# Batch 0's scores from two matmuls a block on keys and maxima in place, a fourth exponentials' buffer, value sums in another bank, and a new written order

## The chip, the cores and the metric

One core of a Trainium2 chip runs the kernel. The time is the device time of one launch in microseconds (us); lower is better. The engines named below are TensorE (PE in the profile, with its weight loads as PEld), VectorE (DVE), ScalarE (ACT), GpSimd (POOL) and SyncE (SP), whose queue starts every DMA here.

## The reference

Two stages follow each other, in float32, on 4 batches, 8 heads, 768 positions, head width 64:

```python
k_sum = k.reshape(B, H, nb, 32, D).max(axis=3)        # maxima of blocks of 32 keys
v_sum = v.reshape(B, H, nb, 32, D).mean(axis=3)       # means of blocks of 32 values
scores_l = scale * q @ k.T, kept where |i - j| < 16   # local window
scores_s = scale * q @ k_sum.T + log(32)              # 24 block scores
a = softmax over [scores_l, scores_s]
x = a @ [v, v_sum]                                    # to 4 x 768 x 512
theta = x @ w_theta
y = w_tok_r @ (x * cos(theta)) + w_tok_i @ (x * sin(theta))
u = x + y
out = u + max(u @ w_ch, 0)
```

Queries, keys, w_theta and w_tok_i are multiplied by 8 first, and the four weight matrices arrive as float64 and are turned into float32 on the core.

## The kernel before, in words

There are 24 attention tiles (4 batches of 6 tiles of 128 positions). A tile is two groups g of 64 positions. A group sees a row of NK = 118 keys: first NB = 24 block maxima, then NL = 94 neighbouring keys.

For a tile the steps are: `scores` (matmuls named s<-k,q, line 522: 16 matmuls of 64x64 weights and 118 columns, 32 instructions in the profile since a float32 matmul is two); the softmax in `att_half` (line 558 on DVE with the mask, line 562 exponentials on ACT); `turn` (line 571, sixteen transposes of the exponentials into banks pa0 and pa1, whose copies of line 577 fill two more buffers of tag "e"); `products` (line 545, exponentials times values v, 32 instructions); `norm_half`; `turn_tile` (line 604, four transposes of the tile into bank t, copied out to x); `theta_tile` (line 635 for batch 0 in whole float32, line 640 later in split halves xh, xl), sine and cosine on ACT, and the multiplication with the tile (line 670, only DVE). `mix_step` (line 698) and `mix_fast` (line 813) multiply by the token weights, and `out_batch` (line 918) by w_ch.

In batch 0 the rows of 118 keys are put together on the core: `copy` (line 499, on ACT or POOL) copies for each tile the 94 keys of each group and the 24 maxima from ks into a buffer k, of which there are two. In the later batches a DMA (k<-kg) brings the keys and only the first two tiles copy maxima. The block means of the values are summed on PE for batch 0 (line 449, x<-vn, into bank pa0), go to a buffer vs on ACT (line 472), and from there by four copies a batch (line 494) into the four v buffers.

Five matmuls on an idle buffer (line 378, t<-zu) stand in the PE queue's first part; nobody reads their result.

The order of all instructions on all engines is written out: `ORDER` is a list of operation numbers, and a letter behind a number chooses the engine (p, a, d, g for PE, ACT, DVE, POOL). Each engine runs its own part of that list in order. `SWITCH` and the other costs in `Program` served to find the order and are not read when the kernel is built.

## Time and profile before

| what | us |
|---|---|
| median of 3 runs | 438.94 (438.0 to 439.17) |
| the profiled execution | 436.4 |
| its span, from the first to the last event | 434.7 |
| TensorE busy in it | 423.7 (97%) |
| DVE, ACT, POOL busy | 357.9, 282.0, 187.8 |

The profiled execution is 1.7 us longer than its span, and 2.5 us below the median of the runs. TensorE is busy nearly all the time, so the profile is read for the few places where it waits and for what its instructions cost next to each other. The granted clock of TensorE is over 90% in each of the profile's 40 slices.

### The profile page before, as it was taken

The page shows a single profiled execution, that of the slowest core. Times are in us where ns is not written, and L with a number is a line of the kernel's source. Part 1 is how long each engine was busy: PE and PEld are TensorE (multiplying, and loading weights), DVE is VectorE, ACT ScalarE, POOL GpSimd, SP SyncE. Part 2 cuts the span into 40 slices and gives each one's busy share as a digit, 9 for nine tenths or more (in the row PEclk, how much of TensorE's full clock was granted, in tenths as well). Part 3 has the DMA queues.
Part 4 walks back from the last instruction along what each step waited for, and adds up shares of the span by engine and source line. Part 5 has one row for each costly group of instructions (what it writes and reads, how often), then busy time and mean ns, then how long its engine had stood idle before and what let it go on. Part 6 is the DMA issues. An engine that isn't in the chain of part 4 may idle for free.

```text
span 434.7 us, 10048 instructions
## 1 busy us (share of the span) xinstructions
PE 423.7 (97%) x3682; PEld 350.2 (81%) x3682; DVE 357.9 (82%) x958; ACT 282.0 (65%) x616; POOL 187.8 (43%) x193
## 2 busy tenths in 40 slices
PE   6999999999999999999999999999999999999996
PEld 1465565566888888888888898999899899999996
DVE  4899999878687597867667987576888999999996
ACT  1899988686685697868396683588944355554330
POOL 2536311678873425257242555451362220253361
PEclk9999999999999999999999999999999999999999
DMA  7999977978975877786779978772368598300357
GB/s 309 385 352 315 340 258 255 255 231 253 301 256 146 247 226 225 225 239 197 205 245 287 285 226 244 246 235 93 112 221 334 166 335 273 99 18 2 109 199 255
DMA packets 76320, 100.06 MB, mean 230 GB/s; under 512 B 23024, under 2 KB 58864, under 8 KB 76272
## 3 DMA queue, kind: packets, MB, share of 16 engines
q1 hardware_dynamic: 76272, 99.43, 71.3%
q8 instruction: 29, 0.48, 0.5%
q14 instruction: 19, 0.16, 0.1%
HBM read 75.82 MB, written 23.59 MB: 229 GB/s over the span
## 4 chain that ended last, share of the span: by engine, by line
PE 80%; DMA 9%; DVE 7%; ACT 2%; issue 1%; SPq 1%; POOL 0%; POOLq 0%; DVEq 0%; ACTq 0%
PE m L813 20%; PE m L698 17%; PE t L640 11%; PE c L918 7%; PE m L918 6%; PE pa L545 5%; PE s L522 4%; DMA v<-vg 2%; PE pa L571 2%; PE t L604 2%; DMA wt<-wtr 2%; DMA q<-qg 1%; PE t L635 1%; DVE f L408 1%; DMA k<-kg 1%; DMA f<-kT 1%
## 5 line engine op out<-in xcount | busy, mean ns | idle before, releaser
L813 PE MATMUL m<-wt,hl 128*128 128x384 f32 x504 | 96.0, 339 | 1.5 <-ACT hl L308 0.8
L813 PEld LDWEIGHTS m<-wt,hl 128*128 128x128 f32 x504 | 88.0, 188 | 5.2 <-ACT hl L308 1.1
L698 PE MATMUL m<-wt,hl 128*128 128x512 f32 (+1 forms) x432 | 84.3, 340 | 0.0
L698 PEld LDWEIGHTS m<-wt,hl 128*128 128x128 f32 x432 | 68.6, 188 | 10.7
L562 ACT ACTIVATE e<-e,st 128x118 f32<-128x118 f32 x192 | 63.5, 388 | 13.6 <-DVE st L558 12.9
L317 POOL TENSOR_TENSOR hl<-zu,hl 128x512 fp32r<-128x512 f32 x24 | 32.5, 1354 | 45.9 <-DVE st L588 15.4
L558 DVE CUSTOM_DVE_ANT_0 e<-s,cs 128x118 f32<-128x118 f32 x192 | 45.6, 272 | 5.1 <-PE s L522 3.2
L640 PE MATMUL t<-wth,xh 128*128 128x512 f32 x144 | 45.8, 399 | 0.0
L670 DVE TENSOR_TENSOR zu<-xn,zu 128x512 f32<-128x512 f32 x48 | 36.9, 780 | 2.4 <-ACT zu L664 2.2
L698 PE MATMUL m<-wt,zu 128*128 128x512 f32 (+1 forms) x96 | 32.8, 488 | 0.0
L726 POOL TENSOR_TENSOR f<-f 128x192 f32<-128x192 f32 x25 | 16.2, 650 | 35.9 <-DMA f<-f_scratch 8.2
L308 ACT CAST hl<-zu 128x512 fp32r<-128x512 f32 x30 | 18.5, 618 | 20.0 <-PE m L813 13.0
L545 PEld LDWEIGHTS pa<-v,e 118*64 118x64 f32 x768 | 24.7, 137 | 6.9 <-issue 2.5
L698 PEld LDWEIGHTS m<-wt,zu 128*128 128x128 f32 x96 | 17.9, 190 | 14.8 <-issue 13.4
L545 PE MATMUL pa<-v,e 118*64 118x65 f32 x768 | 28.1, 224 | 0.9 <-ACT e L577 0.7
L653 DVE SCALAR_TENSOR_TENSOR zu<-zu,t 128x512 f32<-128x512 f32 x24 | 16.4, 682 | 15.3 <-ACT zu L651 15.3
L726 POOL TENSOR_TENSOR zu<-zu 128x512 f32<-128x512 f32 x16 | 21.5, 1348 | 16.5 <-DVE zu L726 9.5
L640 PE MATMUL t<-wth,xl 128*128 128x512 f32 x72 | 28.4, 395 | 0.0
L317 DVE TENSOR_TENSOR hl<-zu,hl 128x512 fp32r<-128x512 f32 x36 | 27.5, 765 | 0.3 <-ACT hl L308 0.2
L651 ACT ACTIVATE zu<-t,bmagic 128x512 f32<-128x512 f32 x24 | 16.5, 687 | 17.3 <-PE t L640 15.5
L522 PE MATMUL s<-k,q 64*64 64x118 f32 x768 | 25.6, 268 | 2.2 <-DMA q<-qg 1.6
L577 ACT COPY e<-pa 118x512 f32<-118x512 f32 x29 | 16.4, 585 | 16.8 <-PE pa L571 16.5
(181 smaller groups left out, 897.2 us busy)
## 6 DMA issues: line engine op xcount, KB each, us to landing
wt<-s_scratch SPq DMA_DIRECT2D x48, 384.0 KB, 4.7
v<-vg SPq DMA_DIRECT2D x48, 195.0 KB, 4.9
s_scratch<-f SPq DMA_DIRECT2D x24, 384.0 KB, 3.5
k<-kg SPq DMA_DIRECT2D x18, 376.0 KB, 5.2
q<-qg SPq DMA_DIRECT2D x24, 256.0 KB, 5.1
wt<-wti SPq DMA_DIRECT2D x6, 768.0 KB, 10.8
wt<-wtr SPq DMA_DIRECT2D x6, 768.0 KB, 10.2
f<-kT SPq DMA_DIRECT2D x12, 384.0 KB, 4.0
```

Of the source, the lines that this page charges most:

```text
L308: nc.scalar.copy(dst(), src())
L317: lambda e: V[e].tensor_tensor(dst(), src(), hi().bitcast(F32), op=ALU.subtract), reads, writes, due, port=BOTH)
L522: mm(0.79 * len(pairs) / NP, [lambda p=p, g=g, h=h: nc.tensor.matmul(sc[h].get()[ROW[g], p], q.get()[ROW[h], p, ROW[g]], k.get()[ROW[h], p ...
L545: mm(2 * 0.433 + scores[0] + (0.2 if scores[0] else 0.0), [lambda n=n, g=g, a=a: nc.tensor.matmul(xa[a].get()[ROW[g], n], turned[g].get()[ ...
L558: op({"DVE": 0.205}, lambda eng, n=n: nc.vector.tensor_tensor_reduce(e()[:, n], sc[n % 2].get()[:, 2 * a + n // 2], mask(m), -SCALE, 3.0e3 ...
L562: op({"ACT": 0.288}, lambda eng, n=n: nc.scalar.activation(e()[:, n], e()[:, n], AF.Exp, bias=st.get()[:, n:n + 1], scale=-1.0), [(st, n)] ...
L640: calls = [lambda t=t, xx=xx, k=k, c=c: nc.tensor.matmul(th.get(), xx.get()[:, c], w_th[c].get()[:, k], start=(c == 0 and t == 0), stop=(c ...
L670: op({"DVE": c_dve(DM, "two")}, lambda e, z=z, hc=hc: nc.vector.tensor_tensor(z(), xn[b, i].get().rearrange("p h d -> p (h d)")[:, None, h ...
L698: nc.tensor.matmul(acc[th](), zz, w[:, TT[th]], start=(s == 0 and r == 0 and t == 0 and (th == 0 or c == 0)), stop=(s == NT - 1 and r == 1 ...
L726: lambda e: V[e].tensor_tensor(dst(), x(), y(), op=ALU.add if sign > 0 else ALU.subtract), reads, writes, due, port=BOTH)
L813: calls = [lambda ref=ref, tt=tt, z=z, s=s, j=j, t=t, x=x, k=k, bank=bank, first=first: nc.tensor.matmul(bank[j].get()[:, :HT], z.get()[:, ...
L918: calls = [lambda k=k, t=t, x=x, y=y: nc.tensor.matmul(to.get(), weights[n][x][0]()[:, k, j * P:(j + 1) * P], operands[n].get()[:, y, k], ...
```

## The change

In batch 0 no buffer k is filled. A block of scores (one pair of heads, one group) comes from two matmuls: one reads the 94 keys where the DMA put them, and one reads the 24 maxima in ks; they write the two column ranges of the same row in the score bank. There are 32 matmuls a tile instead of 16, in batch 0's six tiles alone.

The buffer vs is gone: the means go straight into the first v buffer, and three copies a batch fill the others. Its place goes to a fourth buffer of tag "e". Batch 0's value sums are accumulated in the mixing bank m0 instead of pa0. From the seventh tile on `turn_tile` reads the bank t once (to x), and xh and xl are made from x in SBUF. Two steps may now run on a second engine: rounding theta on DVE, and the multiplication with the tile on POOL. `ORDER` is a new list; in it half of the 48 multiplications of line 670 have gone to POOL.

```diff
 ORDER = """
-8 31 23 0g 17 18 25 27 29 1 24 2 9 39 86 10 26 3 44 28 30 4 32 33 46 45g 47g 50 5 19 35 49 6 48g 7g 87d 51 79 11g 60 12 185 61
...
+0g 15 1g 79 8g 23 2 17g 3 9 80 39 25 31 27 29 81g 33 18 19 82 83 11g 20 24 4 35 26 10 12 5 28 30 21 6g 7 43 32 22 72 44 45 53
...
-            A1=13, T1=10, PREP=5, QB=2, VSPE=1, VB=4, KB=2, STR=2, WARM=5, SP0=1, FUSE=99, RELOAD=2, RT=6, RM=6, XA=6, XB=2, ZU=5, HL=4, EB=3, TAU_A=8.2, TAU_M=4,
+            A1=13, T1=10, PREP=5, QB=2, VSPE=1, VB=4, KB=2, STR=2, WARM=5, SP0=1, FUSE=99, RELOAD=2, RT=6, RM=6, XA=6, XB=2, ZU=5, HL=4, EB=4, TAU_A=8.2, TAU_M=4,
...
-            pv = Ref(ps, [P, NP, P], tag="pa0")
+            pv = Ref(*((pm, [P, DM], F32, "m0") if b == 0 else (ps, [P, DM], F32, "pa0")))
...
-        vs = Ref(apool, [NB, H, DV], tag="vs")
+        vbuf[b] = [Ref(apool, [NB + VL, H, DV], tag="v", bufs=K["VB"]) for _ in range(K["VB"])]
+        first = vbuf[b][0]
...
-            if 2 * i + g < K["VB"]:
+            if 0 < 2 * i + g < K["VB"]:
...
-            if i < K["KB"]:
+            if b > 0 and i < K["KB"]:
                 copy(lambda pp=pp: k.get()[:, pp, :, :NB], lambda pp=pp, n=len(r): ks.get()[:, pp, None].broadcast_to((P, n, 2, NB)), 2 * len(r) * NB,
-            if b == 0:
-                for h in range(r.start // 2, (r.stop + 1) // 2):
-                    for g in range(2):
-                        w = slice((2 * i + g) * QT, (2 * i + g) * QT + NL)
-                        copy(lambda g=g, h=h: k.get()[:, 2 * h:2 * h + 2, g, NB:], lambda h=h, w=w: keys[0][h].get()[:, :, w],
...
         def scores(pairs):
-            mm(0.79 * len(pairs) / NP, [lambda p=p, g=g, h=h: nc.tensor.matmul(
-                sc[h].get()[ROW[g], p], q.get()[ROW[h], p, ROW[g]], k.get()[ROW[h], p, g], start=True, stop=True)
...
+            def block(p, g, h, cols, keys_of):
+                return lambda: nc.tensor.matmul(sc[h].get()[ROW[g], p, cols], q.get()[ROW[h], p, ROW[g]], keys_of(), start=True, stop=True)
...
+                near = [slice((2 * i + g) * QT, (2 * i + g) * QT + NL) for g in range(2)]
+                calls += [block(p, g, h, slice(NB, NK), lambda p=p, g=g, h=h: keys[0][p // 2].get()[ROW[h], p % 2, near[g]]) for g in range(2) for h in range(2)]
+                calls += [block(p, g, h, slice(0, NB), lambda p=p, h=h: ks.get()[ROW[h], p]) for g in range(2) for h in range(2)]
...
-            hi_op(x_h.get, tx.get, DM, [tx], [x_h], due, psum=True)
-            op({"DVE": c_dve(DM)}, lambda e: nc.vector.tensor_tensor(x_l.get(), tx.get(), x_h.get().bitcast(F32), op=ALU.subtract), [tx, x_h], [x_l], due)
+            hi_op(whole, tx.get, DM, [tx], [(x, i)], due, psum=True)
+            hi_op(x_h.get, whole, DM, [(x, i)], [x_h], due, engines=("ACT", "DVE", "POOL"))
+            lo_op(x_l.get, whole, x_h.get, DM, [(x, i), x_h], [x_l], due)
...
-            op({"DVE": c_dve(DM, "two")}, lambda e, z=z, hc=hc: nc.vector.tensor_tensor(
+            op({"DVE": c_dve(DM, "two"), "POOL": c_pool(DM)}, lambda e, z=z, hc=hc: V[e].tensor_tensor(
```

The DMAs that SP starts first, before the change (zu<-kT are batch 0's keys, x<-vn its values for the sums, wth<-wth the theta weights, wt the token weights):

```order
L302 DMA x<-vn 128x2x512
L302 DMA zu<-kT 128x798 x4
L302 DMA q<-qg 128x512
L302 DMA wth_100<-wth 128x1024
L302 DMA x<-vn 128x2x512 x2
L302 DMA wth_150<-wth 128x1024
L302 DMA q<-qg 128x512
L302 DMA v<-vg 96x520 x2
L302 DMA wth_234<-wth 128x1024
L302 DMA wth_238<-wth 128x1024
L302 DMA q<-qg 128x512
```

And the same place in the changed kernel:

```order
L301 DMA wth_80<-wth 128x1024
L301 DMA zu<-kT 128x798
L301 DMA q<-qg 128x512
L301 DMA zu<-kT 128x798
L301 DMA x<-vn 128x2x512
L301 DMA zu<-kT 128x798 x2
L301 DMA x<-vn 128x2x512 x2
L301 DMA wth_155<-wth 128x1024
L301 DMA q<-qg 128x512
L301 DMA wth_197<-wth 128x1024
L301 DMA v<-vg 96x520 x2
L301 DMA q<-qg 128x512 x2
```

A first part of the theta weights now stands ahead of everything; the first values stand behind the second keys; the queries of tile 3 stand right behind those of tile 2, and the last theta weights behind both.

The start of the PE queue before (s<-k,q scores, t<-zu the idle matmuls, pa<-x,vt the value sums):

```order
L378 MATMUL t<-zu 128x512
L449 MATMUL pa_114<-x,vt 24x512 x2
L522 MATMUL s_121<-k,q 64x118
L522 MATMUL s_123<-k,q 64x118
...
L378 MATMUL t<-zu 128x512
L449 MATMUL pa_114<-x,vt 24x512 x4
```

And in the changed kernel:

```order
L377 MATMUL t<-zu 128x512 x4
L521 MATMUL s_133<-zu,q 64x94
L521 MATMUL s_135<-zu,q 64x94
...
L521 MATMUL s_133<-ks,q 64x24
L521 MATMUL s_135<-ks,q 64x24
...
L449 MATMUL m_151<-x,vt 24x512 x2
L377 MATMUL t<-zu 128x512
```

Four of the five idle matmuls now stand ahead of the first scores (one before) and one behind them (four before, all among the first three tiles), and the first two value sums have moved behind the first half of tile 0's scores.

A round of the PE queue in the middle, before, in batch 1 (pa<-cs,e transposes, pa<-v,e products, t<-cs,xn the tile's transposes, m<-wt,hl mixing):

```order
L698 MATMUL m_1474<-wt,hl 128x256
L571 MATMUL pa_1803<-cs,e 118x64
...
L522 MATMUL s_1828<-k,q 64x118
...
L545 MATMUL pa_1850<-v,e 64x65 x8
L545 MATMUL pa_1859<-v,e 64x65 x8
L604 MATMUL t<-cs,xn 128x128 x4
L698 MATMUL m_1491<-wt,hl 128x512
```

And a round of the changed kernel, in batch 2:

```order
L709 MATMUL m_2195<-wt,hl 128x256
L579 MATMUL pa_2650<-cs,e 118x64
...
L709 MATMUL m_2193<-wt,hl 128x512
...
L612 MATMUL t<-cs,xn 128x128 x4
L553 MATMUL pa_2704<-v,e 64x65 x8
L553 MATMUL pa_2713<-v,e 64x65 x8
L521 MATMUL s_2728<-k,q 64x118
...
L709 MATMUL m_2229<-wt,hl 128x512
```

The scores have gone from between transposes and products to behind the products, and six mixing matmuls stand between the transposes of the exponentials and the tile's transposes. Over the whole queue, transposes of exponentials are followed directly by split mixing or theta matmuls at 2 places before and at 13 now.

## Rows read from the trace of the kernel before

**Rows 1.** The page: each engine's busy time, share of the span, instructions.

```profile
PE 423.7 (97%) x3682; PEld 350.2 (81%) x3682; DVE 357.9 (82%) x958; ACT 282.0 (65%) x616; POOL 187.8 (43%) x193
```

**Rows 2.** What TensorE waited for: us in total, times, longest.

```profile
PE s L522 <- DMA q<-qg: 1.6, 1, 1.6
...
PE m L813 <- ACT hl L308: 0.8, 1, 0.8
PE pa L545 <- ACT e L577: 0.7, 3, 0.4
PE s L522 <- POOL k L499: 0.6, 1, 0.6
PE m L813 <- DVE x L822: 0.6, 1, 0.6
PE pa L545 <- DVE e L577: 0.2, 1, 0.2
```

**Rows 3.** Timeline of TensorE's opening: start, length, what, count, wait before.

```profile
9.73 0.64 PE L522 MATMUL s<-k,q 64*64 64x118 f32 x16 [1.58 <-DMA q<-qg]
10.30 1.12 PE L378 MATMUL t<-zu 128*128 128x512 f32 x2
...
12.97 3.62 PE L449 MATMUL pa<-x,vt 128*24 128x512 f32 x8
16.52 1.04 PE L522 MATMUL s<-k,q 64*64 64x118 f32 x32
...
44.14 1.02 PE L698 MATMUL m<-wt,zu 128*128 128x512 f32 x2
```

**Rows 4.** Timeline of TensorE, one round in batch 1.

```profile
118.75 0.68 PE L571 MATMUL pa<-cs,e 64*118 64x64 f32 x16
119.36 1.04 PE L522 MATMUL s<-k,q 64*64 64x118 f32 x32
120.33 1.15 PE L545 MATMUL pa<-v,e 118*64 118x65 f32 x32
...
121.82 3.42 PE L698 MATMUL m<-wt,hl 128*128 128x512 f32 x18
125.08 0.62 PE L640 MATMUL t<-wth,xh 128*128 128x512 f32 x2
...
125.78 1.20 PE L698 MATMUL m<-wt,hl 128*128 128x512 f32 x6
126.81 0.62 PE L640 MATMUL t<-wth,xh 128*128 128x512 f32 x2
```

**Rows 5.** Timeline of TensorE, the two rounds with mixing behind the transposes.

```profile
226.62 0.68 PE L571 MATMUL pa<-cs,e 64*118 64x64 f32 x16
...
231.46 0.62 PE L640 MATMUL t<-wth,xh 128*128 128x512 f32 x2
...
308.87 0.68 PE L813 MATMUL m<-wt,hl 128*128 128x384 f32 x3
309.48 0.68 PE L571 MATMUL pa<-cs,e 64*118 64x64 f32 x16
...
313.49 0.63 PE L640 MATMUL t<-wth,xh 128*128 128x512 f32 x2
```

**Rows 6.** Timeline of ACT: tile 0's first exponential, tile 2's copy to x.

```profile
12.46 0.39 ACT L562 ACTIVATE e<-e,st 128x118 f32<-128x118 f32 x1 [3.10 <-DVE st L558]
...
39.36 0.60 ACT L308 COPY x<-t 128x512 f32<-128x512 f32 x1
```

**Rows 7.** Groups of ACT: shape, count, busy us, mean ns, idle before.

```profile
L499 ACT COPY k<-zu 128x188 f32<-128x188 f32 x7 | 2.2, 341 | 0.6 <-DMA zu<-kT 0.6
```

**Rows 8.** Timeline of DVE: first maxima, first softmax step.

```profile
5.47 0.95 DVE L445 TENSOR_REDUCE ks<-zu 128x24 f32<-128x768 f32 x1 [3.65 <-DMA zu<-kT]
...
12.14 0.28 DVE L558 CUSTOM_DVE_ANT_0 e<-s,cs 128x118 f32<-128x118 f32 x1 [0.71 <-PE s L522]
```

**Rows 9.** The chain that ended last, in its opening: start, length, what.

```profile
3.23 6.37 DMA q<-qg
```

More of the change, by code (lines that the diff above doesn't have):

```diff
@@ L484, in att_tile @@
             kbuf[b] = []
[L485 removed]
         pr.late, pr.key = K["R_KV"], ("KV", b * NT + i)
[L487 removed]
+        x, ks = xt[b], ksum[b]
         q = Ref(apool, [P, NP, P], tag="q", bufs=K["QB"])
@@ L521, in scores @@
         def scores(pairs):
-            mm(0.79 * len(pairs) / NP, [lambda p=p, g=g, h=h: nc.tensor.matmul(
-                sc[h].get()[ROW[g], p], q.get()[ROW[h], p, ROW[g]], k.get()[ROW[h], p, g], start=True, stop=True)
-                for p in pairs for g in range(2) for h in range(2)], [q] + [(k, (x, y)) for x in pairs for y in ("sum", 0, 1)], [(x, y) for x in sc for y in pairs], due, mode="score")
+            def block(p, g, h, cols, keys_of):
+                return lambda: nc.tensor.matmul(sc[h].get()[ROW[g], p, cols], q.get()[ROW[h], p, ROW[g]], keys_of(), start=True, stop=True)
+            calls, rd = [], [q]
+            for p in pairs:
+                if b > 0:
+                    calls += [block(p, g, h, slice(0, NK), lambda p=p, g=g, h=h: k.get()[ROW[h], p, g]) for g in range(2) for h in range(2)]
+                    rd += [(k, (p, y)) for y in ("sum", 0, 1)]
+                    continue
+                near = [slice((2 * i + g) * QT, (2 * i + g) * QT + NL) for g in range(2)]
+                calls += [block(p, g, h, slice(NB, NK), lambda p=p, g=g, h=h: keys[0][p // 2].get()[ROW[h], p % 2, near[g]]) for g in range(2) for h in range(2)]
+                calls += [block(p, g, h, slice(0, NB), lambda p=p, h=h: ks.get()[ROW[h], p]) for g in range(2) for h in range(2)]
+                rd += [(keys[0][p // 2], p), (ks, p)]
+            mm((0.79 if b > 0 else 1.0) * len(pairs) / NP, calls, rd, [(x, y) for x in sc for y in pairs], due, mode="score")
         products()
```

207 lines of the change are left out of this document (105 added, 102 removed).

## The prediction

> **What bounds the kernel now.** The page comes first: TensorE is busy for 423.7 of 434.7 us [rows 1], so at most 11 us of the span are not its work, and some of those are the launch and the last output. The list of its waits comes second [rows 2]: it names one wait for the first queries (1.6), 0.9 in four short waits for the copied transposes, 0.6 for copied maxima before batch 1's first scores, and 0.8 and 0.6 late in the mixing. Nothing else of weight stands there. The third view is the timeline of the opening [rows 3]: first scores at 9.73, tile 1's scores at 16.52, the raw mixing at 44.14. Between 9.73 and 44.14 TensorE also runs four idle matmuls, 1.05 each: 1.12 in the record, less the 0.07 by which a record reaches into the next (9.73 + 0.64 against 10.30). The reader is to see that there is little waiting to remove, that every added microsecond of matmul counts after 44.14, and that before 44.14 TensorE follows ScalarE: tile 0's first exponential is at 12.46 and tile 2's copy to x ends at 39.96 [rows 6], 27.5 us with hardly a gap.
>
> The sum is made against the profiled execution's span of 434.7; its time is 436.4, and the median of the runs shown is 438.94. I add the difference of spans to the median. What a measurement can tell from no change is 0.3%, here 1.3 us.
>
> **The score matmuls.** A tile's 32 score instructions take 0.97 from start to the products' start, eight on each of four quarters of the array, so 0.121 for 118 columns; the transposes take 0.61 for eight on each half, 0.076 for 64 columns [rows 4]. A line through both gives 0.023 plus 0.00083 a column: 0.101 for 94 columns and 0.043 for 24, together 0.023 more than one of 118, and 0.18 more a tile. From below, the columns are as many as before: 0. From above, a 24-column matmul costs no more than the 64-column row, 0.076: 0.45 a tile. I take 0.2, as the line has it. That is 1.0 us in the five tiles before 44.14 and 0.2 in the sixth.
>
> The Trainium skill, page "TensorEngine Tiling (Array Packing)", section "Instruction Overhead", speaks against the split: a matmul has about 60 cycles of overhead and one column takes as long as 60. By that rule the 24 columns would be priced as 60, 0.073 on the same line, and a tile would cost an estimated 0.42 more, 2.5 us in all six instead of 1.2. No row here has a matmul that small, so it is the upper end that the rule leans to.
>
> **The opening.** Batch 0's DMAs arrive one behind the other. Sizes follow from the shapes (399 KB for a 128x798 tensor, 512, 256). The first keys are there at 5.47 [rows 8], with 911 KB; the queries at 3.23 + 6.37 = 9.60 [rows 9], with 2364 KB: 352 KB/us. In the new order the last keys have 2876 KB, so they land at 11.0 instead of about 9, and their maxima (0.95 on DVE, rows 8) are ready at 12.0. The first half of tile 0's scores can start sooner, at about 9.2 (before 9.73), but the softmax takes both halves: it starts at about 13.0 instead of 12.14 [rows 8]. Tile 1's queries are the same number of bytes down the line in both orders (4668 KB, 16.1), so its scores stay near 16.5.
>
> TensorE's own work from the first scores to the mixing was 34.4 minus 0.7 of waits. Three idle matmuls leave it (3.15), two of six value sums come in (half of the four that took 3.55 from 12.97 to 16.52, rows 3: 1.8), the scores add 1.0: 33.3. From 9.2 that would reach 42.5 with no wait at all. ScalarE decides: it loses six copies in this stretch (2.2 for seven [rows 7], so 1.9) and about 0.3 net of small steps, 25.3 instead of 27.5. It begins at 13.2, and then has nothing ready until the value sums end and tile 0's transposes are through; I charge 1.2 for that. Tile 2's copy then ends at 39.7, and with the same 4.2 as before the mixing starts at 43.9. **Term: -0.25**, between -1.6 (no wait) and +0.7 (ScalarE 1 us later). So the copies, which VectorE and GpSimd no longer serve, and the idle matmuls give back little here: what is late next is ScalarE. The fourth buffer costs nothing and lets exponentials start before a product has read the old ones; its cover is that nothing else used that space. The other cost at nothing is the queries of tile 3, now issued right behind tile 2's: they wait for tile 1's scores, and the last theta weights and two v loads stand behind them on SP. Those weights are needed some 8 us later; were that cover gone, theta of tile 0 would start late by the excess.
>
> **The order in the middle.** In a round before the change, transposes, scores, products and the tile's transposes lie in a row between mixing: 118.75 to 125.08 is 6.33, less 18 mixing matmuls at 0.172 (1.03 for six, 125.78 to 126.81) and less the scores' 0.97 leaves 2.26 [rows 4]. Where mixing stood behind the transposes, 309.48 to 313.49 with nine mixing matmuls leaves 2.46, and 226.62 to 231.46 with twelve leaves 2.78 [rows 5]. The new form thus costs 0.20 to 0.52 more a round, and the scores, now behind the products, I add at their plain 0.97. The changed order has 13 such places instead of 2. **Term: 11 x 0.20 = +2.2**; the lower row of the two, since the other one holds a short wait. The new places before 44.14 are none.
>
> The same page of the Trainium skill, section "Key Properties", says that a change of the tiling mode drains TensorE. The rows agree that a change costs: three mixing matmuls before transposes take 0.61 (308.87 to 309.48, rows 5) instead of 0.52. Counted by that rule alone, 112 changes of tile shape become 121, and the term would be an estimated 9 x 0.09 = 0.8 instead of 2.2; I keep whole rounds, since they hold what a drain is not.
>
> **The waits after 44.14.** They sum to 2.2: 0.6 and 0.2 for maxima and transposes, 0.8 and 0.6 late [rows 2]. The first should go: half of the multiplications of line 670 leave DVE, which is the engine that makes the maxima, and batch 1's k buffers no longer wait for batch 0's scores to read them. The 0.2 goes too, since mixing now covers the copies between transposes and products. Of the late 1.4 I leave 0.8: the ring of four hl buffers is as it was, but w_ch matmuls are now mixed in earlier. **Term: -1.4**, between -2.2 and 0.
>
> **The sum.** -0.25 + 0.2 + 2.2 - 1.4 = +0.75: a span of 435.4, and 439.7 for the median of runs. That is within 0.3%.
>
> **Rivals.** *Faster.* The fourth buffer and the lighter ScalarE let TensorE run the opening without a wait: the mixing starts at 42.5 (1.4 sooner than forecast), and the late waits go altogether (0.8 more). That gives -1.45 from before, 437.5. For it speaks that three of the waits in [rows 2] are ScalarE's copies and that it loses 1.8 us of copies; against it, that the softmax starts later and the bytes are the same. Chance 0.27.
>
> *Slower by the order.* Each of the 11 rounds costs 0.52, as the row at 226.62: 3.5 more than forecast, 443.2. From 0.25 a round on, the change is over 1.3 us slower. For it, that it is one of only two rows of this form; against it, that the other reads 0.20. Chance 0.19.
>
> *Slower by the small matmuls.* At 0.45 a tile the sixth tile adds 0.25 and the five others 1.25, of which the waits for ScalarE hide a part, most likely half: +0.9 on the forecast, 440.6; it takes the 0.45 and a wait of ScalarE's that is no longer there to be slower by 0.3%. Chance 0.12.
>
> *No change that a measurement shows,* as summed: 0.42, with its own range of 437.8 to 440.2.
>
> **The numbers.** The cases give faster 0.27, within 0.3% 0.42, slower 0.31. The bounds added up go from -3.9 (mixing at 42.5, 0.8 for the order, no late wait, scores at 0) to +6.6 (mixing at 44.8, 0.52 a round, all late waits, scores at 0.45). I cut both ends, which need every bound at once: 436.2 to 442.8.
>
> **What would show it.** The first scores near 9.2 but the softmax near 13; the raw mixing between 43 and 45. Score groups of batch 0 about 1.15 from start to start instead of 0.97. Rounds with mixing behind the transposes 0.2 longer. No wait for k before batch 1's scores; one late wait for hl. The prediction is wrong if the mixing starts before 42.5 or after 45, if a round of the new form costs under 0.1 or over 0.3 more, if batch 0's scores take over 1.4, or if TensorE waits anew in batches 1 to 3, where it hardly waited.

## The result: 443.75 us, slower by 1.3%

The changed kernel takes 443.75 us (median of 6 runs, 442.13 to 445.15), the kernel before 437.96 on the same chip (6 runs, 436.6 to 439.17): a ratio of 1.0132, interval 1.0104 to 1.016. The forecast of 439.7 with "no change that a measurement shows" was wrong, and its range ended at 442.8. The time is that of the rival "slower by the order" (443.2), but not for its reason, as the runs show.

The first two profiles differ by more than the medians (spans 443.1 and 434.7, 8.4 us), because the one of before fell on one of its fastest executions and that of the changed kernel on the slowest of its six (445.15). Both kernels were therefore profiled again (`b_again`, `a_again`: spans 437.3 and 440.9, 3.6 us). What is said of sizes below goes by this second pair, with the first beside it; the medians differ by 5.8. The page of the changed kernel, first engines, then the queue that brings instructions (packets, MB, share), against [rows 1]:

```profile
span 443.1 us, 10396 instructions
PE 427.8 (97%) x3874; PEld 353.9 (80%) x3874; DVE 362.4 (82%) x961; ACT 279.4 (63%) x579; POOL 191.6 (43%) x195
q8 instruction: 30, 0.49, 0.5%
```

TensorE has 192 matmuls more (6 tiles x 32, a float32 matmul being two) and is busy 4.1 us longer. Its list of waits, which answers to [rows 2]:

```profile
PE pa L553 <- ACT e L585: 2.7, 2, 1.9
...
PE t L612 <- DVE zu L664: 1.6, 2, 0.9
PE m L824 <- issue: 1.0, 1, 1.0
PE s L521 <- DMA k<-kg: 0.7, 1, 0.7
PE m L824 <- ACT hl L307: 0.7, 1, 0.7
PE pa L579 <- ACT xn L601: 0.5, 2, 0.3
PE m L709 <- POOL zu L681: 0.4, 1, 0.4
```

The wait for copied maxima is gone, as forecast. In its place stand waits that the list before does not have: for bank t, which must be read before the next transposes of the tile (zu L664), for normed tiles (xn), for the DMA of keys (0.5 in `b_again` too), and an "issue" of 1.0 in the last mixing, where the engine waits for nothing that the profile names. The opening, to be held against [rows 3]:

```profile
8.12 0.39 PE L521 MATMUL s<-zu,q 64*64 64x94 f32 x8
...
9.47 1.88 PE L449 MATMUL m<-x,vt 128*24 128x512 f32 x4
...
16.56 0.39 PE L521 MATMUL s<-zu,q 64*64 64x94 f32 x8
...
17.80 0.68 PE L579 MATMUL pa<-cs,e 64*118 64x64 f32 x16
...
25.55 0.30 PE L553 MATMUL pa<-v,e 118*64 118x65 f32 x2 [1.93 <-ACT e L585]
...
27.22 2.08 PE L646 MATMUL t<-xh,x 128*128 128x512 f32 x2
29.23 0.59 PE L521 MATMUL s<-zu,q 64*64 64x94 f32 x8
...
31.10 1.12 PE L646 MATMUL t<-xl,x 128*128 128x512 f32 x2
...
35.45 0.66 PE L612 MATMUL t<-cs,xn 128*128 128x128 f32 x4 [0.89 <-DVE zu L664]
...
47.80 7.90 PE L709 MATMUL m<-wt,zu 128*128 128x512 f32 x24
```

First scores stand at 8.12 (forecast 9.2), a tile's scores take 16.56 to 17.80 = 1.24, the mixing starts at 47.80 (forecast 43 to 45). Tile 1's products wait 1.93 for exponentials, and then two theta matmuls take 2.0 instead of about 0.95, and the scores at 29.23 take 1.87. The windows there (length, then PE, weight loads, DVE, ACT, POOL, granted clock, DMA share, GB/s) tell why:

```profile
24.00:26.00 2.00, 0.30 (x2) 0.19 (x2) 1.28 (x7) 1.69 (x4) 0.62 (x1) 1.00 1.10 323
26.00:28.00 2.00, 1.83 (x31) 1.51 (x32) 1.61 (x8) 1.43 (x5) 0.00 (x0) 0.80 0.96 322
28.00:30.00 2.00, 2.00 (x26) 0.78 (x28) 1.17 (x5) 1.58 (x4) 0.60 (x1) 0.50 0.99 391
```

After a stretch in which TensorE worked 0.30 of 2 us its granted clock falls to half, 1.2 instead of 2.4 GHz.

The forecast let ScalarE set the pace of the opening. From its first exponential to the end of its copy of tile 2 to x, ScalarE (ACT, the fourth of the busy times) worked for 26.70 of 27.50 us before and works for 25.21 of 30.10 now:

```profile
12.46:39.96 27.50, 26.70 (x344) 14.92 (x344) 26.38 (x115) 26.70 (x68) 13.82 (x26) 1.00 1.02 342
```

```profile
13.78:43.88 30.10, 25.98 (x474) 16.69 (x474) 25.92 (x105) 25.21 (x61) 6.85 (x10) 0.94 1.00 331
```

So it has less work, and it waits 4.9 us instead of 0.8. Its longest waits here are for loads of weights, 1.73 for theta's (xl) and 1.00 for a token weight (f), and 1.13 are for VectorE. The copies that tile 1's products wait for stand right behind the first of these (24.88):

```profile
24.31 0.67 ACT L399 ACTIVATE xl<-wth 128x512 f32<-128x512 f32 x1 [1.73 <-DMA wth<-wth]
...
43.29 0.59 ACT L307 COPY x<-t 128x512 f32<-128x512 f32 x1
```

The mixing follows the end of that copy by 3.9 us (4.2 before). A round in the middle, which answers to [rows 4]:

```profile
206.40 0.68 PE L579 MATMUL pa<-cs,e 64*118 64x64 f32 x16
207.02 1.31 PE L709 MATMUL m<-wt,hl 128*128 128x512 f32 x6
208.17 0.60 PE L612 MATMUL t<-cs,xn 128*128 128x128 f32 x4
208.70 1.15 PE L553 MATMUL pa<-v,e 118*64 118x65 f32 x32
209.78 1.04 PE L521 MATMUL s<-k,q 64*64 64x118 f32 x32
210.75 1.31 PE L709 MATMUL m<-wt,hl 128*128 128x512 f32 x6
211.90 0.39 PE L651 MATMUL t<-wth,xh 128*128 128x512 f32 x1
```

206.40 to 211.90 is 5.50; less twelve mixing matmuls at 0.172 and 0.97 for the scores it is 2.47, 0.21 more than the 2.26 of the form before.

The second pair, `b_again` and then `a_again`: the first raw mixing; then `a_again`'s longest waits from the mixing to 390 us.

```profile
45.91 4.46 PE L698 MATMUL m<-wt,zu 128*128 128x512 f32 x13
```

```profile
46.82 3.60 PE L709 MATMUL m<-wt,zu 128*128 128x512 f32 x10
```

```profile
PE m L824 <- issue: 1.0, 1, 1.0
PE s L521 <- DMA q<-qg: 0.7, 1, 0.7
PE t L612 <- DVE zu L664: 0.7, 1, 0.7
PE pa L553 <- DMA v<-vg: 0.5, 1, 0.5
```

In `b_again` the waits there are 0.9 for hl, 0.6 each for copied maxima and xl, and 0.5 each for keys and x. In `a_again` ScalarE works for 24.85 of 28.92 us from its first exponential to its copy of tile 2 (13.97 to 42.89), with 2.6 of waits for weights and 1.1 for VectorE.

Of the 3.6 us between the two spans, 0.9 lie before the mixing, 3.4 between it and the last 288 matmuls for w_ch (382.75 before, 387.03 after), and the tail gives 0.7 back. TensorE's waits in the middle sum to 3.16 in `b_again` and 4.10 in `a_again`, so 0.9 of the 3.4 is waiting and 2.4 is longer work. In the first pair it is 3.7, 5.3 (2.3 of it waits, 3.1 work) and -0.6. The work in the middle differs least between the pairs; the opening and the waits vary more from execution to execution.

### The profile page after: what moved, and what is told of

Read it like the earlier page. It is cut to its first block, busy times and chain, and to the rows that moved or that the text cites. A ratio compares the mean times of both kernels' runs of the same rounds, so it can differ in the third digit from the quotient of the medians.

```text
span 443.1 us, 10396 instructions
## 1 busy us (share of the span) xinstructions
PE 427.8 (97%) x3874; PEld 353.9 (80%) x3874; DVE 362.4 (82%) x961; ACT 279.4 (63%) x579; POOL 191.6 (43%) x195
## 4 chain that ended last, share of the span: by engine, by line
PE 73%; DVE 14%; DMA 8%; issue 2%; ACT 1%; SPq 1%; POOL 0%; DVEq 0%; ACTq 0%
PE m L709 17%; PE m L824 17%; PE t L651 10%; PE c L929 7%; PE m L929 5%; PE s L521 5%; PE pa L553 4%; DMA f<-vT 2%; PE pa L579 2%; PE t L612 2%; DVE f L407 2%; DVE wt L410 2%; DMA v<-vg 2%; DMA zu<-kT 1%; DMA f<-kT 1%
## 5 line engine op out<-in xcount | busy, mean ns | idle before, releaser
L709 PE MATMUL m<-wt,hl 128*128 128x512 f32 (+1 forms) x432 | 87.0, 342 | 0.1
L570 ACT ACTIVATE e<-e,st 128x118 f32<-128x118 f32 x192 | 64.5, 388 | 18.2 <-DVE st L566 17.9
L316 POOL TENSOR_TENSOR hl<-zu,hl 128x512 fp32r<-128x512 f32 x25 | 33.8, 1355 | 38.7 <-DVE hl L316 12.5
L681 POOL TENSOR_TENSOR zu<-xn,zu 128x512 f32<-128x512 f32 x24 | 32.2, 1345 | 37.8 <-ACT zu L675 15.6
L709 PE MATMUL m<-wt,zu 128*128 128x512 f32 (+1 forms) x96 | 33.7, 492 | 0.4 <-POOL zu L681 0.4
L553 PEld LDWEIGHTS pa<-v,e 118*64 118x64 f32 x768 | 24.9, 137 | 9.7 <-issue 5.9
L709 PEld LDWEIGHTS m<-wt,zu 128*128 128x128 f32 x96 | 17.5, 190 | 14.5 <-issue 12.2
L737 POOL TENSOR_TENSOR f<-f 128x192 f32<-128x192 f32 x26 | 17.3, 665 | 26.8 <-DVE hl L316 7.9
L307 ACT CAST hl<-zu 128x512 fp32r<-128x512 f32 x28 | 17.0, 617 | 18.9 <-PE m L824 10.4
L651 PEld LDWEIGHTS t<-wth,xh 128*128 128x128 f32 x144 | 24.2, 188 | 2.7 <-issue 0.2
L585 ACT COPY e<-pa 118x512 f32<-118x512 f32 x34 | 19.1, 586 | 8.9 <-PE pa L579 8.9
L664 DVE SCALAR_TENSOR_TENSOR zu<-zu,t 128x512 f32<-128x512 f32 x24 | 16.4, 684 | 7.4 <-ACT zu L662 7.0
```

The lines of the kernel that those rows point to most:

```text
L316: lambda e: V[e].tensor_tensor(dst(), src(), hi().bitcast(F32), op=ALU.subtract), reads, writes, due, port=BOTH)
L553: mm(2 * 0.433 + scores[0] + (0.2 if scores[0] else 0.0), [lambda n=n, g=g, a=a: nc.tensor.matmul(xa[a].get()[ROW[g], n], turned[g].get()[ ...
L570: op({"ACT": 0.288}, lambda eng, n=n: nc.scalar.activation(e()[:, n], e()[:, n], AF.Exp, bias=st.get()[:, n:n + 1], scale=-1.0), [(st, n)] ...
L585: lambda e, t=t, g=g: (nc.scalar.copy if e == "ACT" else nc.vector.tensor_copy)(t.get()[:NK], tp[g].get()[:NK].rearrange("k n q -> k (n q) ...
L651: calls = [lambda t=t, xx=xx, k=k, c=c: nc.tensor.matmul(th.get(), xx.get()[:, c], w_th[c].get()[:, k], start=(c == 0 and t == 0), stop=(c ...
L681: op({"DVE": c_dve(DM, "two"), "POOL": c_pool(DM)}, lambda e, z=z, hc=hc: V[e].tensor_tensor(z(), xn[b, i].get().rearrange("p h d -> p (h ...
```

## The experiments

Three questions: what makes the opening late, what the order costs, and what each edit costs by itself. Each ratio is to the kernel before on the same chip. "The mixing" is the start of the first raw mixing; "later waits" are TensorE's waits from there on, summed.

**The opening.** The theories: a *queue* theory (tile 3's early query load delays the weights and values behind it on SP), a *work* theory (the matmuls there simply take longer, and ScalarE is late), and a *clock* theory (fewer idle matmuls among the first tiles let the granted clock fall). Four kernels ran together; `a_again` is the changed kernel without an edit.

> The changed kernel once more, nothing edited, as the measure for the three runs beside it and for how much of its profile comes back. If the opening's loss belongs to the kernel, the trace again has the wait of about 1.9 us before tile 1's products, the stretch at half clock after it (26.7 to 30.3) and the raw mixing near 47.8. If it was an accident of one execution, the mixing starts near 44 to 45 and the time is still about 443.7, and the loss has to be sought after it.

443.18, ratio 1.010 (1.0072 to 1.0128). The mixing starts at 46.82, and the clock does not fall at all in this execution. So the half clock is not needed for being slower; it comes on top.

`a_q3_later` moves tile 3's query load (274) behind theta weights (93) and values (179, 181) on SP:

```diff
-223 274 93 179 181 100 224
+223 93 179 181 100 274 224
```

> The changed kernel with the load of tile 3's queries moved back behind the last theta weights, two v loads and a token weight on SP's queue; nothing else. Queue theory: this load held SP from 13.6 to 17.9 us, the theta weights behind it landed at 24.3, ScalarE waited for them with tile 1's copies behind, TensorE stood 1.9 + 0.3 us and its clock then halved for 3.7 us (1.85 lost). Without it: no wait over 0.8 before tile 1's products, no half clock, mixing at 44 to 44.7 instead of 47.8, a time 3 to 4 us under the changed kernel's (about 440.3). Rival, clock theory: the missing idle matmuls leave gaps of 0.8 to 0.9 that halve the clock anyway: the wait goes but the half-clock stretch stays, mixing near 46. Rival, ScalarE's pace: mixing not before 47.

445.17, 1.0136 (1.0104 to 1.0167), mixing at 49.92: no gain. The theta weights are issued 4.4 us earlier (13.91 instead of 18.35) but reach ScalarE at 23.63, where the two profiles of the changed kernel have 24.31 and 23.44, so the queue theory fell: their place on SP is not what makes them late. The time alone would not show it, since this profile has other losses: the clock is at half from 26.3 to 29.7, and TensorE stands still inside tile 2's scores, where nothing is missing that another engine makes. Timeline, and the window up to the stall:

```profile
22.08 0.36 PE L521 MATMUL s<-zu,q 64*64 64x94 f32 x5
...
24.66 0.30 PE L521 MATMUL s<-zu,q 64*64 64x94 f32 x2 [2.22 <-issue]
```

```profile
0.00:24.65 24.65, 17.50 (x219) 8.32 (x220) 13.58 (x54) 10.74 (x26) 6.62 (x23) 1.00 0.95 311
```

`a_idle_back` puts the idle matmuls (18 to 22) back among the first three tiles (43, 44 the halves of tile 0's scores, 183 tile 1's, 32 to 36 value sums):

```diff
-18 19 20 21 43 32 22 44 34 36 183 61 62 65 226
+18 43 32 19 44 20 34 36 183 61 62 21 65 22 226
```

> The changed kernel with the five idle matmuls at the places of the kernel before (one in front, one behind each half of tile 0's scores, one behind tile 0's transposes, one behind its products); loads as in the changed kernel. Queue theory alone: the products of tile 1 still wait for ScalarE's copies near 25.5, now with 0.9 less idle time ahead; what is gained is at most the clock. Clock theory: with the gap from 23.6 to 25.5 shortened and the gap before tile 0's products filled, the half-clock stretch goes, mixing near 46.0, the time 1.5 to 2 us lower (about 442). If neither: the idle matmuls only add work, mixing at 48 or later and the time up to 1 us higher.

444.22, 1.0131 (1.0101 to 1.016). From 9.35, its first value sums, TensorE is busy for 18.32 of 18.65 us:

```profile
9.35:28.00 18.65, 18.32 (x274) 9.08 (x276) 12.95 (x64) 10.61 (x29) 2.55 (x5) 1.00 0.90 312
```

Yet the mixing starts at 47.87. The clock column (1.00) counts the time ahead of the trace's first clock record as full, and here that record begins at 12.08. Up to there TensorE ran at the lower level: the four value sums take 3.22, against 1.88 in the changed kernel (9.47 above).

```profile
9.35 3.22 PE L449 MATMUL m<-x,vt 128*24 128x512 f32 x4
```

With three idle matmuls more between the first scores and the mixing (1.05 each), TensorE's gaps are filled, and now ScalarE waits for TensorE: 3.3 of the 28.95 us from its first exponential to its copy of tile 2. So the run trades one wait for another and gains nothing; it does not tell what holds the opening of the changed kernel. Ahead of the window the queries and maxima kept TensorE waiting for 2.0 and 0.9, as the queries did in [rows 3].

`b_idle_front` gives the kernel before the new places of the idle matmuls:

```diff
-18 32 50 19 51 20 34 36 195 68 69 21 72 22 242
+18 19 20 21 32 50 22 51 34 36 195 68 69 72 242
```

> The kernel before with its idle matmuls at the places of the changed kernel (four in front, one between the halves of tile 0's scores). If ScalarE alone sets the opening (my prediction's step), the mixing starts at 44.1 as before, with waits where the idle matmuls stood: time within 0.3% of before. If TensorE's work sets it, the mixing starts up to 3 us sooner. Clock theory: with the idle matmuls gone from between the tiles, the waits lower the granted clock somewhere between 18 and 35 us, and the mixing starts 0.5 to 2 us later.

438.91, 1.001 (0.9992 to 1.0028), mixing at 46.12 (45.91 in `b_again`). TensorE has three idle matmuls less from the first scores to the mixing, and waits 4.9 us there instead of 2.2: its own work does not set that opening. Idle matmuls alone are worth nothing in it.

`a_idle_two`, run later, moves one of them ahead of tile 0's products (65) and one ahead of its transposes (211), behind which TensorE had waited:

```diff
-18 19 20 21 43 32 22 44 34 36 183 61 62 65 226 200 201 211 204
+18 19 43 32 20 44 34 36 183 61 62 21 65 226 200 201 22 211 204
```

> The changed kernel with two of its four front idle matmuls moved: one ahead of tile 0's products, one ahead of tile 0's turned tile, so into the stretch where TensorE waits for ScalarE's copies before tile 1's products (0.5 to 2.2 us in five traces) and the granted clock was at half for 3.4 us or more behind it in four of the five. Clock theory: no stretch at half clock behind it, mixing at 46 to 46.8, time 0.5 to 1.5 lower (442). Rival, work theory: each idle matmul is 1.05 of TensorE's own, and the time is 0.5 to 2 higher (444 to 445) with mixing at 48; so it was with five at the old places, where the clock stayed up and the mixing came at 47.9 all the same.

444.56, 1.0128 (1.0097 to 1.0159). The clock was at half from 9.8 to 13.2 and from 37.1 to 40.5, elsewhere than in the changed kernel, and the mixing started at 50.45. The clock theory's remedy fails.

**The order.** Operations are numbered alike in these kernels, so that the first 263 (about the opening) can be taken from one list and the rest from the other. `a_old_order` has all edits in the order of before, without the removed operations; `a_open_old` takes only the opening from it, `a_rest_old` only the rest.

```diff
 ORDER = """
-0g 15 1g 79 8g 23 2 17g 3 9 80 39 25 31 27 29 81g 33 18 19 82 83 11g 20 24 4 35 26 10 12 5 28 30 21 6g 7 43 32 22 72 44 45 53
+8 31 23 0g 17 18 25 27 29 1 24 2 9 39 79 10 26 3 28 30 4 32 33 43 5 19 35 6 7g 80d 44 72 11g 53 12 178 54 20 57 45 56 46 81g 47
...
```

> All edits of the code (scores from two matmuls in place, no copies of keys, no buffer vs, four exponentials' buffers, value sums in the mixing bank, the bank t read once), but every operation in the place and on the engine that it had in the kernel before; the operations that are gone are left out of the list. Order theory: the new list is the loss, and the edits cost at most the 0.27 us a tile that the trace shows for the scores, of which the five tiles of the opening hide some: 437.5 to 439.5, ratio 0.998 to 1.003. Rival, edits theory: twice as many matmuls, and twice as many instructions to fetch while the DMA queues are full, cost the opening 3 us: 441 or more, with waits named issue before batch 0's scores or products. A third way: six copies less on ScalarE and sixteen less on GpSimd gain what the matmuls cost and more: 436 or less.

> The changed kernel, with its first 263 operations (all that its list has ahead of the mixing) in the order and on the engines of the kernel before; the rest in the new order. If the loss lies in the opening alone (3.7 us by the first two traces), the time is 440 or less, ratio to before 1.000 to 1.004. If it lies in the order behind 44 us (2.7 for rounds, 2.3 for waits by those traces), the time stays at 442.5 to 443.5. If both, near 441.

> The other half: the changed kernel's opening in its new order, and all that follows in the order of the kernel before. If the loss lies in the opening alone: 442 to 443. If it lies in the middle's rounds and waits: 439 or less, and the rounds behind 100 us have the old form at 0.2 us less each. If both halves cost, this run and the one with the old opening share the 5 us between them, and their sum over before comes to the changed kernel's.

> The kernel before once more, nothing edited, for a second profile of it: the first one was of an execution of 436.4, below the median of its runs. If the first trace is typical, the raw mixing again starts near 44.1 and TensorE's waits after it sum to about 2.2. If the opening varies from one execution to the next, the mixing starts between 44.5 and 46.5, and part of the 3.7 us by which the changed kernel's opening seemed later is not the change's.

| kernel | us | ratio (interval) | mixing | later waits |
|---|---|---|---|---|
| b_again | 438.55 | 1.0001 (0.9972 to 1.003) | 45.91 | 3.2 |
| a_old_order | 448.49 | 1.0212 (1.0177 to 1.0248) | 46.15 | 7.4 |
| a_open_old | 443.01 | 1.009 (1.0055 to 1.0125) | 48.14 | 2.9 |
| a_rest_old | 452.62 | 1.0334 (1.0284 to 1.0385) | 46.80 | 11.1 |

This turned the question round. The edits in the order of before cost 2.1%, and the new list takes 0.8 to 1.1 of that back. Nor is the opening the main part: with either opening the new rest gives 0.9 to 1.3%, with the old rest 2.1 to 3.3%. (In the profile of `a_open_old` the clock record begins at 16.38, so its mixing is late by up to 3.1 us for that alone.) So it was to be asked what the edits cost.

**One part each.** `b_rounds` is the kernel before, with one group of six mixing matmuls in 14 rounds moved up behind the transposes of the exponentials, the new form of round. The PE queue at the first of them:

```diff
 L571 MATMUL pa_1393<-cs,e 118x64
-L522 MATMUL s_1421<-k,q 64x118
...
+L698 MATMUL m_1421<-wt,hl 128x512
+L698 MATMUL m_1423<-wt,hl 128x256
...
+L522 MATMUL s_1430<-k,q 64x118
```

> The kernel before, where in 14 rounds (tiles 8 to 16 and 18 to 22) six mixing matmuls are taken from behind the tile's transposes and put between the transposes of the exponentials and the scores; nothing else moves. My prediction's price of this form is 0.20 a round, the upper one 0.52. With 0.20: 14 x 0.20 = 2.8 us slower, 441, ratio 1.005 to 1.008, and each such round reads 0.2 longer in the timeline. With 0.52: 7 us slower. If the tile mode costs nothing by itself and the loss in rounds came from waits: 438 to 439.

466.12, 1.0596 (1.0553 to 1.064). Such a round without waits:

```profile
124.48 0.68 PE L571 MATMUL pa<-cs,e 64*118 64x64 f32 x16
125.08 1.32 PE L698 MATMUL m<-wt,hl 128*128 128x512 f32 x6
126.34 1.04 PE L522 MATMUL s<-k,q 64*64 64x118 f32 x32
...
128.80 1.53 PE L698 MATMUL m<-wt,hl 128*128 128x512 f32 x7
```

```profile
PE t L640 <- DVE xl L610: 7.9, 10, 1.4
PE m L698 <- DVE x L717: 5.4, 3, 2.0
```

124.48 to 128.80 is 4.32, less 1.03 to 1.045 for the six 3.28, where [rows 4] leave 118.75 to 121.82 = 3.07: +0.21, as in the changed kernel. Fourteen such rounds are 2.9 of the 27.9 us between this span and that of `b_again` (465.2 and 437.3). The waits in the middle sum to 20.7, 17.5 more: scores that come 1.25 later make VectorE's queue, which works in its written order, late for what stands behind them. The other 7.5 are longer work, about 3.3 of it the lower clock (0.98 from 45 to 120, 0.97 from 280 to 340); the rest I have not placed. The form of the round costs 0.2, and it can't be had alone: the other engines' lists must be written for it.

`c_old_x` is `a_old_order` with bank t read twice, as before the change; the other edits remain.

```diff
-            whole = lambda: x.get()[:, :, i * P:(i + 1) * P]
-            hi_op(whole, tx.get, DM, [tx], [(x, i)], due, psum=True)
-            hi_op(x_h.get, whole, DM, [(x, i)], [x_h], due, engines=("ACT", "DVE", "POOL"))
-            lo_op(x_l.get, whole, x_h.get, DM, [(x, i), x_h], [x_l], due)
+            hi_op(x_h.get, tx.get, DM, [tx], [x_h], due, psum=True)
+            op({"DVE": c_dve(DM)}, lambda e: nc.vector.tensor_tensor(x_l.get(), tx.get(), x_h.get().bitcast(F32), op=ALU.subtract), [tx, x_h], [x_l], due)
```

> As the run in the old order, but the bank t is read as in the kernel before (xh from the bank, xl as bank minus xh on DVE, x from the bank); the other edits stay. The old order with all edits lost 10 us, nearly all behind 46 us, where DVE's xl and xn end waits that were not there. Theory: the longer chain bank, x, xh, xl (one more step of 0.6 us ahead of theta) is what the old order has no room for: without it 437.5 to 440. Rival: the means written straight into the first v buffer hold that buffer early, so that v loads and the queue behind them come late: the time stays at 444 or more. Where the time falls between, both count.

442.07, 1.0064 (1.0037 to 1.0091), later waits 3.7 instead of 7.4. The single read, which the forecast had not priced, is over half of what the edits cost in this order.

`b_x_once` is that edit the other way, the removed lines above alone put into the kernel before. `b_x_noport`, run later, makes xh and xl without the kernel's rule by which an operation of GpSimd waits for such a step of VectorE ahead of it in the list.

> The kernel before with the third edit alone: the bank t read once into x, xh made from x and xl from x and xh (the two copies take the places of the two that read the bank, in that order; xl follows). The difference of the two runs in the old order says 6.4 us for this edit there. If the longer chain ahead of theta is that cost: 442 to 445, with waits for xl of 0.5 to 1.5 before theta. If the cost came from where that run had put the copies: 438 to 439.5.

> The kernel before with the bank t read once, as in the run with that edit alone (0.95% slower), except that the two operations that now read SBUF no longer count for the kernel's rule by which an operation of GpSimd waits for the DVE operation on SBUF ahead of it in the list. If GpSimd's added wait is what that edit cost (3.2 us for xl ahead of a hl at 282, and TensorE's 1.3 for that hl), the time comes back to within 0.3% of before, 438 to 440. If the longer chain, or the slower operations themselves when GpSimd works beside them (the mean of xl rose from 0.69 to 0.84), are the cost, it stays at 442 to 444.

```diff
-            hi_op(x_h.get, whole, DM, [(x, i)], [x_h], due, engines=("ACT", "DVE", "POOL"))
-            lo_op(x_l.get, whole, x_h.get, DM, [(x, i), x_h], [x_l], due)
+            hi_op(x_h.get, whole, DM, [(x, i)], [x_h], due, psum=True)
+            op({"DVE": c_dve(DM)}, lambda e: nc.vector.tensor_tensor(x_l.get(), whole(), x_h.get().bitcast(F32), op=ALU.subtract), [(x, i), x_h], [x_l], due)
```

443.28, 1.0095 (1.0061 to 1.0129), and 442.02, 1.01 (1.007 to 1.013). The groups of xl in `b_again`, `b_x_once` and `b_x_noport` (count, busy, mean ns, idle before):

```profile
L610 DVE TENSOR_TENSOR xl<-t,xh 128x512 fp32r<-128x512 f32 x18 | 12.3, 686 | 6.7 <-ACT x L308 3.6 <-ACT xh L308 3.1
```

```profile
L317 DVE TENSOR_TENSOR xl<-x,xh 128x512 fp32r<-128x512 f32 x18 | 15.2, 844 | 8.0 <-ACT xh L308 7.5
```

```profile
L612 DVE TENSOR_TENSOR xl<-x,xh 128x512 fp32r<-128x512 f32 x18 | 18.5, 1029 | 7.8 <-ACT xh L308 7.5
```

The subtraction takes 686 ns on the mean with one operand in the bank, 844 with both in SBUF, and 1029 with both in SBUF and without the rule. One by one, the 18 of `b_again` take 659 to 692, with an operation of GpSimd beside them or not. With both operands in SBUF those that no operation of GpSimd overlaps take 677 to 694, no longer than before; among the overlapped ones the longest takes 1825 in `b_x_once` and 2217 in `b_x_noport`. With the rule GpSimd stands instead, and TensorE behind it, in `b_x_once`:

```profile
282.11 1.31 POOL L317 TENSOR_TENSOR hl<-zu,hl 128x512 fp32r<-128x512 f32 x1 [3.23 <-DVE xl L317]
```

```profile
283.47 0.45 PE L816 MATMUL m<-wt,hl 128*128 128x384 f32 x1 [1.33 <-POOL hl L317]
```

Either way 1.0%: without that wait the 18 subtractions take 18.5 us instead of 15.2, and the time stays.

`a_x_twice` puts the two reads into the changed kernel with its own order (the diff of `c_old_x`).

> The changed kernel with the bank t read as in the kernel before (xh from the bank, xl on DVE as bank minus xh, x from the bank), each operation in the place that its successor has in the new list. If the edit costs in the new order what it costs in the old (0.95%, 4 us), the time falls to 439 to 440.5, the best version with the other edits. If the new order was made for it and hides it, the time stays at 443. If the bank, held longer, makes theta late, it rises to 445 and TensorE waits for xl or for the bank before theta and before the turned tiles.

444.21, 1.0118 (1.0077 to 1.0159), mixing 48.01, later waits 2.8. In the new order taking the single read back gains nothing that can be measured: that list hides what it costs.

`b_scores_only` gives the kernel before batch 0's new scores alone, with the 27 copies gone; `b_vs_only` gives it the means in the first v buffer, the fourth "e" buffer and bank m0.

```diff
+                near = [slice((2 * i + g) * QT, (2 * i + g) * QT + NL) for g in range(2)]
+                calls += [block(p, g, h, slice(NB, NK), lambda p=p, g=g, h=h: keys[0][p // 2].get()[ROW[h], p % 2, near[g]]) for g in range(2) for h in range(2)]
+                calls += [block(p, g, h, slice(0, NB), lambda p=p, h=h: ks.get()[ROW[h], p]) for g in range(2) for h in range(2)]
```

```diff
-        vs = Ref(apool, [NB, H, DV], tag="vs")
+        vbuf[b] = [Ref(apool, [NB + VL, H, DV], tag="v", bufs=K["VB"]) for _ in range(K["VB"])]
+        first = vbuf[b][0]
```

> The kernel before with the first edit alone: batch 0's scores from two matmuls a block in place and no copies into k for batch 0 (27 operations of ScalarE and GpSimd less); order, buffers and all else as before. If TensorE's added work counts in full: 6 x 0.27 = 1.6 slower, 440, ratio 1.003 to 1.005. If the opening waits for loads and ScalarE anyway: the sixth tile's 0.3 alone, ratio 0.999 to 1.002, mixing at 45.5 to 46. If the copies held the opening: mixing at 44 or sooner, ratio 0.995 to 0.998.

> The kernel before with the buffer vs gone, the means straight in the first v buffer, four exponentials' buffers and batch 0's value sums in the mixing bank; scores, bank t and order as before. In the run in the old order with the bank read as before, one wait of 1.4 for xn stood near 164 us, and a v load of batch 2 has to wait until batch 1's products have read that buffer. If this is the edit's doing, the wait is here too, and the time is 1 to 2.5 over before, 440. If it came with the scores: 438 to 439, no such wait.

439.98, 1.002 (0.9997 to 1.0044), and 441.24, 1.0048 (1.0023 to 1.0073). The scores cost at most 0.4%, and the 27 copies gave nothing back that shows: the mixing is at 47.02, 1.1 later than in `b_again`. The means are no free edit in that order: the first v buffer takes the place of vs, and batch 2's load of it is issued 10 us later, with what stands behind it on SP. In `b_again`, then `b_vs_only`, the load, and a wait of TensorE there that `b_again` has not:

```profile
142.52 0.90 SPq L302 DMA_DIRECT2D v<-vg  x1
```

```profile
152.86 0.33 SPq L302 DMA_DIRECT2D v<-vg  x1
...
163.01 0.67 PE L573 MATMUL pa<-cs,e 64*118 64x64 f32 x15 [1.32 <-DVE xn L597]
```

That the one brings the other was not tried by itself.

`a_one_matmul` is the changed kernel with one matmul of 118 columns of keys in place of 94 and 24; the block maxima are left out of batch 0's scores.

```diff
-                calls += [block(p, g, h, slice(NB, NK), lambda p=p, g=g, h=h: keys[0][p // 2].get()[ROW[h], p % 2, near[g]]) for g in range(2) for h in range(2)]
-                calls += [block(p, g, h, slice(0, NB), lambda p=p, h=h: ks.get()[ROW[h], p]) for g in range(2) for h in range(2)]
+                calls += [block(p, g, h, slice(0, NK), lambda p=p, g=g, h=h: keys[0][p // 2].get()[ROW[h], p % 2, near[g]]) for g in range(2) for h in range(2)]
```

> The changed kernel with one matmul of 118 columns a block in batch 0, all of them keys read in place (the block maxima are left out of batch 0's scores; they are still computed and waited for). It prices the second matmul: the trace shows 1.24 from start to start for a tile of the split form and 0.97 for whole rows, so 0.27 a tile and 1.6 in six. If TensorE's work sets the opening, the mixing starts 1.3 us sooner and the time is 1.6 lower (441.6). If loads and other engines set it: the sixth tile's 0.27 alone, 443. If twice the instructions to fetch are the burden, the waits named issue in the opening go too, and it is 2 us or more.

441.5, 1.0062 (1.0034 to 1.0091), about 1.7 less than `a_again`; 6 x 0.27 is 1.6. The intervals overlap, so the agreement is no proof.

`a_z_dve` sets all 48 multiplications of line 681 to VectorE (24 letters g dropped from `ORDER`, one of them here).

```diff
-222 139 264g 158 338
+222 139 264 158 338
```

> The changed kernel with all 48 multiplications of theta's sine and cosine with the tile on DVE, as before (24 of them are on POOL in the new list); order unchanged. If POOL's 1.35 us against 0.78 is what makes new waits (0.4 for zu at the raw mixing, and what follows), the time falls by 0.5 to 1.5: 441.7 to 442.7. If DVE has no room for 24 x 0.78 = 19 us more in this order, its waits grow and the time rises by 1 to 4: 444 to 447. Same time: it matters to nothing.

448.29, 1.0204 (1.0164 to 1.0244), later waits 8.4, half clock from 25.3 to 32.1. The multiplications on GpSimd are a gain, in this order at least.

No version beat the kernel before. Added up, in the old order, scores 0.20, means and fourth buffer 0.48, single read 0.95 make 1.6%, against 2.1 (1.8 to 2.5) for all together; within the intervals the two agree.

## Why the prediction was wrong

*The opening, -0.25: failed.* It was +0.9 in the second pair and +3.7 in the first. Most of the step held. The scores start early (8.12), the softmax waits for both halves (13.25, forecast about 13.0), tile 1's scores stand at 16.56 (about 16.5), ScalarE's own work is 25.2 and 24.9 us (25.3), and the mixing follows its copy of tile 2 by 3.9 (4.2). What failed is the wait set between, 1.2 us in which ScalarE has nothing ready: it measured 4.9 and 4.1. The step let ScalarE wait for value sums and transposes alone; in the traces it waits for loads of weights (2.7 and 2.6) and for VectorE (1.1 in both). So the time of the six copies came back as waiting. TensorE on its side waits 4.4 and 4.2 us between its first scores and the mixing, 0.7 and 2.2 before; 0.9 to 1.0 of it is bank t (35.45 above), where the kernel before has no wait. In the first profile its clock is also at half from 27.2 to 30.6. Less these, its work there is 33.6 us, close to the 33.3 of the sum. Why the weights come late stays open, and so does how much of the first pair's 3.7 is the scatter of executions (44.14 and 45.91 for the same kernel before).

*The scores, 0.2 a tile: a little small.* 1.24 less 0.97 is 0.27, between the line through two widths (0.18) and the estimate of 0.42 by the Trainium skill, page "TensorEngine Tiling (Array Packing)", section "Instruction Overhead". The rival "small matmuls" at 0.45 is out.

*The order, +2.2: right in the price of a round.* Rounds of 2.47 and 3.28 both give +0.21. Work in the middle grew by 2.4 (3.1 in the first pair), with 0.27 of it the sixth tile's scores. That the rest is the rounds alone is not shown: reckoned the same way it is 4.0 more than in `b_again` in `a_old_order` and 2.2 more in `b_x_once`, both with the rounds of before. The rival with 0.52 a round is out, although its time was met. The count of mode changes alone, 0.8, was too little.

*The waits, -1.4: failed, with the wrong sign.* They went up, by 0.9 and 2.3. The wait for copied maxima did go, but loads of keys, queries and values of 0.5 to 0.7 each stand in its place (of these `b_again` has the keys); bank t makes TensorE wait again near 277; and the late pair, forecast to shrink from 1.4 to 0.8, is 1.65 in the first profile after (0.69 for hl, 0.96 "issue"). The step took the waits of before one by one and let each go; it did not ask what is late next.

*What was costed at nothing.* The fourth buffer and the query load of tile 3 were named with covers. The second cover, that the theta weights behind that load are needed some 8 us later, did not hold, since ScalarE waited 1.73 us for them; but moving the load back in `a_q3_later` gained nothing. The single read of bank t and the means in the first v buffer had no term at all, and are the two dearest edits in the order of before (1.0 and 0.5%). In the new order the first is hidden, as `a_x_twice` shows. Here lies the answer to where a gain went: the new list does give back 0.8 to 1.1 of 2.1%, but to edits that cost more than they bring. The tail's -0.7 was not foreseen either.

Two bounds of the range don't add up: by its own terms the lower end is -3.0, not -3.9, and the upper 6.8, not 6.6. The 443.75, which is 4.8 over the 438.94 of the sum, lies inside these bounds and outside the range cut from them.

In the second pair the sum reads 0.9 (opening) + 2.4 (work) + 0.9 (waits) - 0.7 (tail) = 3.6, rounded parts, where the forecast had +0.75.

## What to carry to other kernels

Price an edit and the order apart: run the edits in the old order first, since a new list can hide what they cost. Here, with TensorE busy for 97%, copies taken off another engine gave nothing back that could be measured, while new waits of an engine that works in written order were passed on; ask of every removed wait what is late next, and forecast how long an engine will wait as carefully as how long it will work. Profile a kernel twice before a difference of under 1% is put to a place.

## What was unexpected of the hardware

**Fetching instructions.** TensorE stalled for 2.22 us at 24.66 in `a_q3_later` and for 0.76 at 32.11, with no releaser. By their places in the PE queue 449 and 705 matmuls and weight loads come before them, 256 apart, and the queue that brings instructions moves 0.49 MB in 30 packets, 16 KB each. Batch 0 now has 384 such instructions more, while data transfers fill the DMA engines (share 0.95). The Trainium skill, page "Runtime: NRT & Kernel Launch", section "Instruction fetch mechanics", tells of blocks of 16 KiB or 256 instructions, at a cost "mostly hidden". The spacing and size agree; hidden it was not here. The times agree too: in `a_q3_later` the first two packets on that queue are under way from 21.85 to 23.25 and from 29.55 to 30.63, and TensorE goes on 1.4 and 1.5 us behind their ends. In the two profiles of the changed kernel the same instructions start 1.3 us or more behind the ends of theirs. So the stalls are late blocks; what makes a block late, the data transfers or something else, no run took apart.

**VectorE beside GpSimd.** A subtraction of 128x512 took 659 to 692 ns with one operand in a PSUM bank, beside GpSimd or not. With both in SBUF it took 677 to 694 where no operation of GpSimd ran beside it, and up to 2217 where one did. Reading a bank twice was the cheaper way in the order of before.

**Executions differ in the opening.** The same kernel started the mixing at 44.14 and 45.91, the changed one at 47.80 and 46.82, once with a fall of the clock and once without. When the clock first rises differs as well. With four idle matmuls in front it is at its upper level from 5.6 to 8.2 us on in eight traces, with one in front from 7.7 to 16.4 us on in eleven. Before that an idle matmul takes 2.0 us instead of 1.05 (`a_open_old` at 11.32).
